# A spectral filter beside an MLP block on one core: four more warm-up matmuls and another order in step one

## The chip, the cores and the metric

The kernel runs on one NeuronCore of a Trainium2 chip. Its engines are called as in the profile: PE multiplies matrices (PEld is its loading of weights), DVE, ACT and POOL work element by element, SP issues the DMAs. The metric is the time of one execution on the device in microseconds. Lower is better.

## The reference

For x of 2048 tokens by 448 features, with all numbers in float32:

```python
xn = layernorm(x)
out = x + A(xn, w_r, w_i) + B(xn, w1, w2, w3, w4)

def A(x, w_r, w_i):                       # a filter in the frequency domain
    X = rfft2(x) * (w_r + 1j * w_i)       # over tokens and features
    return irfft2(X)

def B(x, w1, w2, w3, w4):
    h = gelu(layernorm(x) @ w1)
    hs = shift(h) @ w2                    # quarters of h moved by +1, -1, +2, -2 tokens
    x1 = x + hs
    return x1 + gelu(layernorm(x1) @ w3) @ w4
```

w3 is 448 by 1792 and w4 1792 by 448. gelu is its tanh form.

## The kernel before

Tokens lie in 16 blocks b of 128 rows: row a of block b is token 16 a + b + 2 (modulo 2048). Two blocks share a tile `xt[p]`, p = b // 2, of 128 by 2 by 448 float32 numbers, on which all results are added up. Float32 matrices are multiplied in three float16 passes: each operand is split into a high half, made by ACT, and a low half, the rest, made by DVE (`PASS`: high by high, high by low, low by high).

The kernel is one stream of instructions per engine. A scheduler lays out each engine's order when the kernel is built, by priorities and by edges written out by hand, and the chip then executes every engine's list strictly in that order. `behind(key)` is such an edge: what is issued in its block comes, on each engine, after the instruction of the same engine noted under that key. It orders an engine's queue and is no wait between engines. Waits between engines come from the data alone.

The stages, in order of time:

1. Start. `warm_up(WARM)` multiplies zeros (`wps`), while x and the weights are loaded. Then the first layer norm (`norm1`), sums of squares of w1 from which a power of two as its scale is found (`powers`, pm, L259), transposes of x on PE (L384), the product with w1 (L415), gelu, the shift, the product with w2 (`w2_tile`, L474). All loads and the transposes by DMA go through SP's queue.
2. The second layer norm, `ln2`, once for two or four blocks: DVE's statistics, centred copies by POOL and ACT (L495, L497), then for each block a scaled high half by ACT (L504), a low half by DVE (L505, L507) and a transpose by DMA (L509) into `x2all`. The last call is for blocks 12 to 15. Pairs 6 and 7 of the MLP read them.
3. The MLP over pairs G of blocks. Its unit (G, fp), fp 0 to 6, has two parts. `front` multiplies with w3 (L395, 22 matmuls of 256 columns into one bank), then come gelu (L724) and the halves hf by ACT (L726) and DVE (L727). `back` multiplies hf with w4 and sums up in two banks acc (L806, 12 matmuls of 448 columns). The fronts run two units ahead of the backs (`AH`). When fp is 6, DVE adds acc to `xt` (L813), which frees the banks. The unit's ACT and DVE instructions are noted as ("f", G, fp), its last matmul as ("m", G, fp). `mlp([0])` comes first, then `mlp([1, 2])`, then the others beside the later stages.
4. Step one of the transform, beside `mlp([1, 2])`. `do_fold(b)` loads x again for two blocks (xf), normalises it (ACT, L536), and POOL folds the features (L542 to L545) into f. `step1_in` splits f into xh (ACT L552, DVE L553), four buffers. `step1(b)` multiplies it with the transform over the 128 rows (L562, 12 matmuls into a bank ps), and ACT (L566) and DVE (L567) write the two halves y. There are two banks ps, so that each pair of blocks needs those of the pair before emptied. `PACE` says behind the last matmul of which unit the pair of blocks 2 i and 2 i + 1 is multiplied, `FOLD` behind which unit it is folded.
5. Also beside `mlp([1, 2])`: `unscale(p)` loads x once more (loads, two halves of a staging space) and sets xt[p] = xt[p] * scale + x on DVE (L515), for p 1 to 7. `w_scale` loads the filter's eight parts (wl, two halves of another space) and takes the largest magnitude of each on DVE (`absmax`, L270 by its helper). `w_scale_end` makes a power of two from the eight. `w4_sums` prepares three parts of w4 for a later stage.
6. The 16 chunks of the transform over tokens with the filter (`chunk_a`, `chunk_b`, `chunk_z`, `chunk_c`) beside pairs 3 and 4, the inverse (`inv_a`, `inv_b`), and pairs 5 to 7 of the MLP.

What sets the order around the change: `between`, called after each front of `mlp([1, 2])`, issues an unscaling or a part of w4 behind the unit that `EARLY` names. The maxima stand behind the units of `WMAX`. The loads' DMAs are issued in program order with no edge, and SP executes its list in order.

Of the kernel before, what the change touches and what calls it, by code (L numbers as in the profile page):

```python
# [25 lines left out]
TURN = [3, 1, 0, 2]  # L26
DONE = {c: [c - 2] for c in range(2, 12)} | {12: [10, 13], 13: [11, 12, 14, 15]}
FIRST = 2
WARM = 24
ZPRE = 2.0 ** -7  # L30
UPRE = 2.0 ** -3
VPRE = 2.0 ** -3
EPS = 1e-5
AH = 2
PACE = [(1, 0), (1, 1), (1, 2), (1, 4), (1, 5), (2, 0), (2, 1), (2, 3)]
FOLD = [(0, 6), (1, 0), (1, 1), (1, 3), (1, 4), (1, 6), (2, 0), (2, 2)]
PIN = [("a3",), ("a3",), ("a3",), ("a3",)]
WMAX = [(1, 4), (1, 5), (1, 6), (2, 0), (2, 1), (2, 2), (2, 3), (2, 4)]
EVAC, FILL = 0, 100000
DH = D // 2  # L40
SEVEN = {5: [0, 4, 5], 6: [0, 4, 5, 1, 2, 3], 7: [0, 1, 2, 4, 5]}
# [83 lines left out]
def body(tc, nc, x, wf, w1, w2, w3, w4, c_g, c_n, c_small, out):  # L125
# [50 lines left out]
    def stage(name, n, side, dtype=F32):  # L176
        t = pw.tile([128, 1808], F32, tag=f"stage{side}", bufs=1, name=name)
        return (t if dtype is F32 else t.bitcast(dtype))[:, :n]
# [90 lines left out]
    def absmax(out_, in_):  # L269
        V.tensor_reduce(out=out_, in_=in_, axis=AX.X, op=ALU.max, apply_absolute_value=True)  # L270
# [98 lines left out]
    @contextlib.contextmanager  # L369
    def behind(*key):  # L370
        key = key if len(key) > 1 else key[0]
        with contextlib.ExitStack() as st:
            for i in after[key]:
                st.enter_context(tc.issue_after(i))
            yield
# [99 lines left out]
        V.scalar_tensor_tensor(out=xb(b), in0=xb(b), scalar=cs[:, CS[b]:CS[b] + 1], in1=pm[:, :D],  # L475
                               op0=ALU.mult, op1=ALU.add)

    def ln2(bs, engines):

        n, b0 = len(bs), bs[0]  # L480
        mv = stats([xb(b) for b in bs], f"b{b0}")
        a = pc.tile([128, 4], F32, tag="vb", bufs=2, name=f"vb{b0}")[:, :n]
        r = pc.tile([128, 4], F32, tag="vs", bufs=2, name=f"vs{b0}")[:, :n]
        o, y = [], []
        nm = pc.tile([128, 4], F32, tag="nm", bufs=2, name=f"nm{b0}")[:, :n]
        P.tensor_scalar(out=nm, in0=mv[:, :n, 0], scalar1=-1.0, scalar2=None, op0=ALU.mult)
        for m in range(0, n, 2):
            w = stage(f"y{b0 + m}", 8 * 448, (b0 + m) // 2 % 2, F16)
            o.append(w[:, 0:4 * D].bitcast(F32).rearrange("p (i n) -> p i n", i=2))
            y.append(w[:, 4 * D:8 * D].rearrange("p (i n) -> p i n", i=2))  # L490
            for i in range(2):
                e = engines[m + i]
                c = nm[:, m + i:m + i + 1]
                if e is A:
                    A.activation(out=o[-1][:, i], in_=xb(b0 + m + i), func=AF.Identity, bias=c)  # L495
                else:
                    e.tensor_scalar(out=o[-1][:, i], in0=xb(b0 + m + i), scalar1=1.0, scalar2=c,  # L497
                                    op0=ALU.mult, op1=ALU.add)
        V.tensor_scalar(out=a, in0=mv[:, :n, 1], scalar1=eps12, scalar2=None, op0=ALU.add)
        rsqrt(r, a, n, f"b{b0}")  # L500
        for i in range(n):
            b, h, x_ = b0 + i, y[i // 2][:, i % 2], o[i // 2][:, i % 2]
            k = r[:, i:i + 1]
            u = A.activation(out=h[:, 0:D], in_=x_, func=AF.Copy, scale=k)  # L504
            V.scalar_tensor_tensor(out=h[:, 448:512], in0=x_[:, 384:448], scalar=k, in1=h[:, 384:448],  # L505
                                   op0=ALU.mult, op1=ALU.subtract)
            v = V.scalar_tensor_tensor(out=h[:, 512:896], in0=x_[:, 0:384], scalar=k, in1=h[:, 0:384],  # L507
                                       op0=ALU.mult, op1=ALU.subtract)
            d = SY.dma_start_transpose(out=x2all[b // 4][:, :, 128 * (b % 4):128 * (b % 4) + 128], in_=h)  # L509
            after[f"b{b0}"] = u.ins, v.ins, d.ins  # L510

    def unscale(p, part):
        t = part.rearrange("p (b n) -> p b n", b=2)
        SY.dma_start(t, xv[:, at_token(2 * p):at_token(2 * p) + 2])
        return lambda: V.scalar_tensor_tensor(out=xt[p], in0=xt[p], scalar=p12, in1=t, op0=ALU.mult, op1=ALU.add)  # L515
# [40 lines left out]
    def step1(b):  # L556
        t = xh_buf[b % 4]
        pm = bank("sp", f"ps1_{b}")
        for q in range(4):
            for n, (xi, ri) in enumerate(PASS):  # L560
                o = xi * 452 + 113 * q
                T.matmul(pm[:, 128 * q:128 * q + 128], t[:, o:o + 128], cR[ri][:, 128 * (q % 2):128 * (q % 2) + 128],  # L562
                         start=n == 0, stop=n == 2)
        src = pm.rearrange("p (q h k) -> p q h k", h=2, k=4)
        y = [Ya[:, p, :, :, :, b, :].rearrange("p q c h k -> p (q c) h k") for p in range(2)]
        A.activation(out=y[0], in_=src, func=AF.Copy)  # L566
        V.tensor_tensor(out=y[1], in0=src, in1=y[0], op=ALU.subtract)  # L567

    sc = pc.tile([128, 4], F32, name="sc")

    def w_scale():
        wm = pc.tile([128, 8], F32, name="wm")
        t = stage("wl", 8 * DF, 1)
        for c in range(8):
            h = t[:, 4 * DF * (c % 2):4 * DF * (c % 2) + 4 * DF]
            SY.dma_start(h, wf.rearrange("c (p r) n -> (c p) (r n)", r=8)[:, 4 * DF * c:4 * DF * (c + 1)])
            with behind("f", *WMAX[c]):
                absmax(wm[:, c:c + 1], h)
        return wm

    def w_scale_end(wm):
        t = pc.tile([128, 4], F32, name="wt")
        V.tensor_reduce(out=t[:, 0:1], in_=wm, axis=AX.X, op=ALU.max)
        pt = bank("sp", "wpt")
        T.transpose(pt[0:1, 0:128], t[:, 0:1], ident)
        V.tensor_reduce(out=t[0:1, 1:2], in_=pt[0:1, 0:128], axis=AX.X, op=ALU.max)
        V.tensor_scalar(out=t[0:1, 1:2], in0=t[0:1, 1:2], scalar1=2.0 ** -20, scalar2=None, op0=ALU.max)
        pb = bank("sp", "wpb")
        T.matmul(pb[:, 0:1], ones[0:1], t[0:1, 1:2], start=True, stop=True)
        e = pc.tile([128, 3], I32, name="we")  # L590
        V.tensor_copy(out=t[:, 2:3], in_=pb[:, 0:1])
        V.tensor_single_scalar(e[:, 0:1], t.bitcast(I32)[:, 2:3], 0x7F800000, op=ALU.bitwise_and)
        V.tensor_single_scalar(e[:, 1:2], e[:, 0:1], 0x7F800000, op=ALU.bitwise_xor)
        V.tensor_scalar(out=sc[:, 0:1], in0=e.bitcast(F32)[:, 1:2], scalar1=ZPRE, scalar2=None, op0=ALU.mult)
        for h in range(2):
            V.tensor_scalar(out=sc[64 * h:64 * h + 64, 2:3], in0=sc[64 * h:64 * h + 64, 0:1], scalar1=2.0 * h - 1.0,
                            scalar2=None, op0=ALU.mult)
        V.tensor_scalar(out=sc[:, 1:2], in0=e.bitcast(F32)[:, 0:1], scalar1=2.0 ** -21 / (ZPRE * UPRE * VPRE),
                        scalar2=s12[:, 0:1], op0=ALU.mult, op1=ALU.mult)
        V.tensor_scalar(out=sc[:, 3:4], in0=sc[:, 1:2], scalar1=p12, scalar2=None, op0=ALU.mult)  # L600
# [146 lines left out]
    def w4_sums(j, part):  # L747

        t = part.rearrange("p (k n) -> p k n", n=DH)
        SY.dma_start(t.rearrange("p (f k) n -> p f (k n)", f=2), w4v[:, 2 * j:2 * j + 2])  # L750

        def go():
            for o, i, k, op in ((3, 3, 1, ALU.subtract), (1, 1, 0, ALU.subtract),
                                (0, 3, 0, ALU.add), (2, 2, 0, ALU.subtract)):
                V.tensor_tensor(out=t[:, o], in0=t[:, i], in1=t[:, k], op=op)
            split_w(w4t[j][:, 0], w4t[j][:, 1], t, s4)
        return go
# [228 lines left out]
    ln2(range(8, 12), [P, A, P, A])  # L986
    for b in range(12, 16):
        w2_tile(b)
    ln2(range(12, 16), [P, A, P, A])
    close("p1")  # L990
    close("pr")

# [6 lines left out]
    for i in range(4):  # L999
        P.memset(xh_buf[i][:, 904:], 0.0)  # L1000
    loads = stage("loads", 1808, 0)
    EARLY = {(1, 0): 1, (1, 1): 2, (1, 3): 3, (1, 5): 4, (1, 6): 5, (2, 1): 6, (2, 2): 7,
             (2, 3): "4", (2, 4): "5", (2, 5): "0"}

    def between(G, fp):
        if (G, fp) in EARLY:
            k, n = EARLY[G, fp], list(EARLY).index((G, fp))
            part = loads[:, 896 * (n % 2):896 * (n % 2) + 896]
            go = w4_sums(int(k), part) if isinstance(k, str) else unscale(k, part)
            with behind("f", G, fp):  # L1010
                go()

    mlp([1, 2], hook=between, ahead=AH, tags=("mm", "tr"))
    for b in range(0, NB, 2):
        do_fold(b)
        step1_in(b)
        step1_in(b + 1)
        with behind("m", *PACE[b // 2]):
            step1(b)
            step1(b + 1)  # L1020
    with behind("X", 14):
        wm = w_scale()
    close("pfd")
    with behind("m", 2, 4):
        w_scale_end(wm)
    pst = pool("pst", side="right")
    zb = [pst.tile([128, 4 * DF + 16], F16, name=f"zb{i}") for i in range(2)]
    for i in range(2):
# [64 lines left out]
```

## Time and profile before

| | us |
|---|---|
| three runs | 412.36, 412.37, 414.42 |
| median | 412.37 |
| the profiled execution | 414.05 |
| its span, first to last instruction | 412.2 |

The profile is of one execution, the one of 414.05 us. All times of its rows are counted from the start of its span. The page's first part gives busy times and their share of the span. A row of the timeline has the start, the duration, the engine, the line of the kernel, the operation, what it writes and reads, and a count where like instructions are merged; in brackets stands how long the engine had been idle and what ended that. A group has its busy time, the mean of one in ns, and the idle time ahead of it. A line of the waits has the engine, what it waited for, the sum in us, how often, and the longest. A helper's line stands for all its callers.

### The profile page before, as it was taken

How to read it: one execution, taken by the hardware profiler on the slowest of the kernel's cores; microseconds unless marked ns; L12 is line 12 of the kernel's file. 1: busy time of each engine (PE TensorE's matmuls, PEld its weight loads, DVE VectorE, ACT ScalarE, POOL GpSimd, SP SyncE). 2: the span in 40 equal slices, each digit the busy share in tenths (PEclk: the TensorE clock that was granted, in tenths of full speed). 3: DMA queues.
4: the chain of work that ended last, by engine and by line, in shares of the span. 5: the costliest groups of instructions: out<-in, count | busy, mean ns of one | idle time of the engine just before them, and what ended most of it. 6: DMA issues, size and time to landing. Idle time of an engine off the chain costs nothing.

```text
span 412.2 us, 8724 instructions
## 1 busy us (share of the span) xinstructions
PE 401.3 (97%) x3389; PEld 298.0 (72%) x3389; DVE 333.9 (81%) x702; ACT 255.8 (62%) x434; POOL 100.9 (24%) x173
## 2 busy tenths in 40 slices
PE   6999999999999999999999999999999999999996
PEld 2655545755658677777787888877777779998995
DVE  5878998999775858987798888956799998966645
ACT  4679789982567857565498888954453453553331
POOL 7688520110035866420011221110000000000000
PEclk9899999999999999999999999999999999999999
DMA  8976985479297557435355556610021012100101
GB/s 272 377 278 128 245 170 146 81 122 198 54 238 208 173 173 233 139 131 143 84 147 152 147 142 161 163 32 14 0 91 68 25 67 82 56 23 0 46 2 45
DMA packets 54596, 52.07 MB, mean 126 GB/s; under 512 B 35678, under 2 KB 48542, under 8 KB 54556
## 3 DMA queue, kind: packets, MB, share of 16 engines
q1 hardware_dynamic: 54556, 51.53, 46.0%
q8 instruction: 26, 0.43, 0.4%
q14 instruction: 14, 0.11, 0.1%
HBM read 38.28 MB, written 3.67 MB: 102 GB/s over the span
## 4 chain that ended last, share of the span: by engine, by line
PE 60%; DMA 2%; issue 1%; DVE 1%; POOL 0%; SPq 0%
PE pw L395 24%; PE acc L806 16%; PE side L776 4%; PE acc L776 3%; PE pu L665 3%; PE pe L686 2%; PE pp L620 2%; PE px L637 2%; PE py L707 2%; DMA wl<-wf 2%; PE ps L562 1%; DVE wm L270 0%; POOL xr L543 0%; POOL f L545 0%; DVE y L567 0%
## 5 line engine op out<-in xcount | busy, mean ns | idle before, releaser
L395 PE MATMUL pw<-x2mem,w3p 128*128 128x256 f16 x1232 | 150.6, 273 | 0.0
L395 PEld LDWEIGHTS <-w3p 128*128 128x128 f16 x1232 | 119.3, 98 | 19.9
L806 PE MATMUL acc<-w4p,hf 128*128 128x448 f16 (+1 forms) x516 | 105.6, 348 | 0.7 <-ACT hf L726 0.7
L806 PEld LDWEIGHTS <-hf 128*128 128x128 f16 x516 | 49.6, 98 | 37.6 <-ACT hf L726 1.0
L724 ACT ACTIVATE pw<-pw,pe 128x512 f32<-128x512 f32 x42 | 27.4, 653 | 29.4 <-PE pw L395 29.4
L727 DVE SCALAR_TENSOR_TENSOR hf<-pw,h,hf 128x512 f16<-128x512 f32 x42 | 31.3, 745 | 12.8 <-ACT hf L726 12.7
L415 PE MATMUL pw<-w1p,xT 128*128 128x448 f16 x176 | 35.5, 356 | 1.1 <-DVE xT L389 0.6
L474 PE MATMUL pw<-w2p,h 128*128 128x448 f16 x176 | 35.6, 353 | 0.9 <-DMA h<-x2mem 0.8
L646 POOL TENSOR_TENSOR z<-te 128x450 f32<-128x450 f32 x16 | 15.7, 982 | 70.3 <-DVE te L644 70.3
L415 PEld LDWEIGHTS <-xT 128*128 128x128 f16 x176 | 17.2, 99 | 18.3 <-ACT xT L388 1.2
L726 ACT ACTIVATE hf<-pw,h 128x512 f16<-128x512 f32 x42 | 28.8, 686 | 1.8 <-PE acc L806 0.8
L474 PEld LDWEIGHTS <-h 128*128 128x128 f16 x176 | 16.9, 98 | 17.1 <-DMA h<-x2mem 2.3
L742 ACT ACTIVATE hz<-g,h 128x896 f16<-128x896 f32 x14 | 14.6, 1042 | 22.6 <-DVE g L739 22.5
L776 PEld LDWEIGHTS <-hz 128*128 128x128 f16 x294 | 28.2, 98 | 0.4
L627 ACT ACTIVATE pf<-pp 64x450 f16<-64x450 f32 x32 | 17.4, 543 | 12.4 <-DVE pf L628 8.0
L628 DVE TENSOR_TENSOR pf<-pp,pf 64x450 f16<-64x450 f32 x32 | 19.9, 622 | 3.4 <-ACT pf L627 3.0
L743 DVE SCALAR_TENSOR_TENSOR hz<-g,h,hz 128x896 f16<-128x896 f32 x14 | 16.1, 1149 | 7.6 <-ACT hz L742 7.6
L553 DVE TENSOR_TENSOR xh<-f,xh 128x452 f16<-128x452 f32 x16 | 12.4, 809 | 7.4 <-ACT xh L552 7.4
L642 ACT ACTIVATE te<-px 64x450 f32<-64x450 f32 x32 | 17.3, 541 | 1.2 <-DMA wc<-wf 0.5
L545 POOL TENSOR_TENSOR f<-xr 128x452 f32<-128x452 f32 x16 | 17.5, 1116 | 0.6
L736 ACT ACTIVATE g<-pw,pe 128x512 f32<-128x512 f32 x14 | 9.5, 681 | 10.1 <-PE pw L395 10.0
L690 ACT ACTIVATE e<-pe 128x226 f32<-128x226 f32 x16 | 5.8, 360 | 16.0 <-DVE vh L700 9.0
(188 smaller groups left out, 716.5 us busy)
## 6 DMA issues: line engine op xcount, KB each, us to landing
wc<-wf SPq DMA_DIRECT2D x32, 225.0 KB, 3.6
wl<-wf SPq DMA_DIRECT2D x8, 450.0 KB, 4.2
xt<-x SPq DMA_DIRECT2D x8, 448.0 KB, 7.4
xf<-x SPq DMA_DIRECT2D x8, 448.0 KB, 3.7
loads<-x SPq DMA_DIRECT2D x7, 448.0 KB, 4.2
out<-xt SPq DMA_DIRECT2D x13, 224.0 KB, 1.9
w3raw<-w SPq DMA_DIRECT2D x3, 896.0 KB, 11.1
gn<-c_g SPq DMA_DIRECT2D x16, 128.0 KB, 3.1
```

The source lines that it names most:

```text
L395: T.matmul(ps_out, wp[:, wi + t, cols], xT[:, xi + t, tok], start=t == 0 and wi + xi == 0, stop=t == 3 and wi == 4)
L415: T.matmul(pm[:, :D], xTs[g][:, xi + t, 128 * i:128 * i + 128], w1p[:, wi + t], start=t == 0 and p == 0, stop=t == 3 and p == 2)
L474: T.matmul(pm[:, :D], h[:, k], w2p[:, w], start=n == 0, stop=n == 10)
L545: P.tensor_tensor(out=f[:, :, k:k + 2].rearrange("p b s d -> p s b d"), in0=u[:, :, 0], in1=u[:, :, 1], op=op)
L627: A.activation(out=hi, in_=src, func=AF.Copy)
L628: V.tensor_tensor(out=lo, in0=src, in1=hi, op=ALU.subtract)
L642: A.activation(out=e[64 * h:64 * h + 64], in_=px_[64 - 64 * h:128 - 64 * h, :2 * DF], func=AF.Copy)
L724: A.activation(out=pm, in_=pm, func=AF.Gelu_apprx_tanh, scale=r3)
L726: i = A.activation(out=h[:, 0], in_=pm, func=AF.Copy, scale=h3)
L727: j = V.scalar_tensor_tensor(out=h[:, 1], in0=pm, scalar=h3, in1=h[:, 0], op0=ALU.mult, op1=ALU.subtract)
L776: m = T.matmul(to, h[:, hi, 128 * blk:128 * blk + 128], b[wi], start=new and n == 0, stop=n == 2 and (last if blk in (2, 5, 3, 0) else end ...
L806: m = T.matmul(to, h[:, hi, o:o + 128], w4p[0][:, wi, f, r], start=first and f % 2 == 0 and n == 0, stop=end and f % 2 == 1 and n == 2, sk ...
```

## The change

Six edits.

- `WARM` is 28 in place of 24.
- `PACE`: the first five pairs are multiplied a unit later, (1, 1), (1, 2), (1, 3), (1, 5), (1, 6) in place of (1, 0), (1, 1), (1, 2), (1, 4), (1, 5). The last three keep their units.
- The unscalings of tiles 3 to 7 and the eight maxima leave the units of `EARLY` and `WMAX`. They are issued right after a pair of step one, on DVE behind the low half y of the pair's second block: none for the pair 0, tile 3 behind the pair 1, up to tile 7 behind the pair 5 (`AFTER`); part 0 behind the pair 0, then 1, 2, 3 and 4, 5, 6, 7 (`WMAX`). Their loads are issued at the same place of the program. Tiles 1 and 2 stay behind the units (1, 0) and (1, 1).
- `w4_sums` of the parts 4, 5 and 0 stays behind the units (2, 3), (2, 4) and (2, 5).
- `w_scale_end` comes behind the last matmul of (2, 3) in place of (2, 4).
- The last call of `ln2` has its four scaled copies (L504) behind the ACT instruction of the unit (0, 6).

```diff
-WARM = 24
+WARM = 28
-PACE = [(1, 0), (1, 1), (1, 2), (1, 4), (1, 5), (2, 0), (2, 1), (2, 3)]
+PACE = [(1, 1), (1, 2), (1, 3), (1, 5), (1, 6), (2, 0), (2, 1), (2, 3)]
-WMAX = [(1, 4), (1, 5), (1, 6), (2, 0), (2, 1), (2, 2), (2, 3), (2, 4)]
+WMAX = [[0], [1], [2], [3, 4], [5], [6], [7], []]
+AFTER = [[], [3], [4], [5], [6], [7], [], []]
...
-    def ln2(bs, engines):
+    def ln2(bs, engines, late=None):
...
-            u = A.activation(out=h[:, 0:D], in_=x_, func=AF.Copy, scale=k)
+            with behind(*late) if late else contextlib.nullcontext():
+                u = A.activation(out=h[:, 0:D], in_=x_, func=AF.Copy, scale=k)
...
-        V.tensor_tensor(out=y[1], in0=src, in1=y[0], op=ALU.subtract)
+        after["y", b] = (V.tensor_tensor(out=y[1], in0=src, in1=y[0], op=ALU.subtract).ins,)
...
-    def w_scale():
-        wm = pc.tile([128, 8], F32, name="wm")
-        t = stage("wl", 8 * DF, 1)
-        for c in range(8):
-            h = t[:, 4 * DF * (c % 2):4 * DF * (c % 2) + 4 * DF]
-            SY.dma_start(h, wf.rearrange("c (p r) n -> (c p) (r n)", r=8)[:, 4 * DF * c:4 * DF * (c + 1)])
-            with behind("f", *WMAX[c]):
-                absmax(wm[:, c:c + 1], h)
-        return wm
+    def w_scale(t, c):
+        h = t[:, 4 * DF * (c % 2):4 * DF * (c % 2) + 4 * DF]
+        SY.dma_start(h, wf.rearrange("c (p r) n -> (c p) (r n)", r=8)[:, 4 * DF * c:4 * DF * (c + 1)])
+        absmax(wm[:, c:c + 1], h)
+
+    wm = pc.tile([128, 8], F32, name="wm")
...
-    ln2(range(12, 16), [P, A, P, A])
+    ln2(range(12, 16), [P, A, P, A], ("f", 0, 6))
...
-    EARLY = {(1, 0): 1, (1, 1): 2, (1, 3): 3, (1, 5): 4, (1, 6): 5, (2, 1): 6, (2, 2): 7,
-             (2, 3): "4", (2, 4): "5", (2, 5): "0"}
+
+    def half(n):
+        return loads[:, 896 * (n % 2):896 * (n % 2) + 896]
 
     def between(G, fp):
-        if (G, fp) in EARLY:
-            k, n = EARLY[G, fp], list(EARLY).index((G, fp))
-            part = loads[:, 896 * (n % 2):896 * (n % 2) + 896]
-            go = w4_sums(int(k), part) if isinstance(k, str) else unscale(k, part)
+        if (G, fp) in ((1, 0), (1, 1)):
+            go = unscale(fp + 1, half(fp))
             with behind("f", G, fp):
                 go()
 
     mlp([1, 2], hook=between, ahead=AH, tags=("mm", "tr"))
+    wl = stage("wl", 8 * DF, 1)
     for b in range(0, NB, 2):
         do_fold(b)
         step1_in(b)
...
         with behind("m", *PACE[b // 2]):
             step1(b)
             step1(b + 1)
-    with behind("X", 14):
-        wm = w_scale()
+        with behind("y", b + 1):
+            for p in AFTER[b // 2]:
+                unscale(p, half(p + 1))()
+            for c in WMAX[b // 2]:
+                w_scale(wl, c)
+    for n, j in enumerate((4, 5, 0)):
+        go = w4_sums(j, half(n))
+        with behind("f", 2, 3 + n):
+            go()
     close("pfd")
-    with behind("m", 2, 4):
-        w_scale_end(wm)
+    with behind("m", 2, 3):
+        w_scale_end()
```

In the changed kernel's lists PE has the same matmuls but for the four. On ACT the gelu and the high half of (0, 6) come ahead of the last four copies, and the gelu of (1, 0) ahead of the first xh. On DVE the low halves y of a pair come ahead of the unscaling and the maximum that follow the pair. On SP the first two loads wl come ahead of the third load for unscaling.

More of the change, by code (lines that the diff above doesn't have):

```diff
@@ L566, in step1, with w_scale_end @@
         A.activation(out=y[0], in_=src, func=AF.Copy)
-        V.tensor_tensor(out=y[1], in0=src, in1=y[0], op=ALU.subtract)
+        after["y", b] = (V.tensor_tensor(out=y[1], in0=src, in1=y[0], op=ALU.subtract).ins,)
     sc = pc.tile([128, 4], F32, name="sc")
-    def w_scale():
-        wm = pc.tile([128, 8], F32, name="wm")
-        t = stage("wl", 8 * DF, 1)
-        for c in range(8):
-            h = t[:, 4 * DF * (c % 2):4 * DF * (c % 2) + 4 * DF]
-            SY.dma_start(h, wf.rearrange("c (p r) n -> (c p) (r n)", r=8)[:, 4 * DF * c:4 * DF * (c + 1)])
-            with behind("f", *WMAX[c]):
-                absmax(wm[:, c:c + 1], h)
-        return wm
-    def w_scale_end(wm):
+    def w_scale(t, c):
[3 more added lines that the diff above has]
+    wm = pc.tile([128, 8], F32, name="wm")
+    def w_scale_end():
         t = pc.tile([128, 4], F32, name="wt")
```

## The prediction

> **What bounds the kernel now.** I read the page first, then PE by stages, then what ended PE's idle times, then the order of time around each of them.
>
> ```profile
> span 412.2 us, 8724 instructions
> PE 401.3 (97%) x3389; PEld 298.0 (72%) x3389; DVE 333.9 (81%) x702; ACT 255.8 (62%) x434; POOL 100.9 (24%) x173
> ```
> ```profile
> 7.50:10.90 3.40, 1.19 (x9) 0.71 (x7) 2.05 (x8) 2.14 (x7) 1.14 (x2) 1.00 1.02 323
> 10.90:14.35 3.45, 3.45 (x17) 2.79 (x16) 3.00 (x9) 3.23 (x7) 1.25 (x2) 0.51 1.05 331
> ```
> ```profile
> 161.65:192.90 31.25, 31.25 (x289) 24.23 (x289) 28.20 (x45) 17.94 (x30) 9.18 (x10) 1.00 0.41 131
> 192.90:404.30 211.40, 211.40 (x2053) 173.83 (x2051) 171.23 (x324) 120.39 (x202) 15.72 (x16) 1.00 0.27 77
> 404.30:412.20 7.90, 4.58 (x37) 3.28 (x34) 3.31 (x6) 1.35 (x2) 0.00 (x0) 1.00 0.17 58
> ```
> ```profile
> PE pm L259 <- DVE pt L257: 2.2, 1, 2.2
> PE ps L562 <- DVE y L567: 1.4, 2, 0.9
> PE acc L806 <- ACT hf L726: 0.7, 1, 0.7
> ```
>
> In the rows by stage the columns are the length, the busy time of PE, weight loads, DVE, ACT and POOL, the granted clock, the DMA share and GB/s. PE is the bound: from 161.65 to 404.30 it isn't idle for a moment, so whatever makes PE reach that point earlier shortens the kernel by as much, as long as its inputs come earlier too. PE is idle 412.2 - 401.3 = 10.9 us. Of this 3.3 lie in the last 7.90 us, 1.2 before the first matmul and 2.2 before the first sum (pm), which waits for the squares of w1 and not for PE. Two other waits are what this change touches: 0.7 at an acc and 1.4 at the ps of step one. About 2.0 us of idle lie elsewhere. Besides, PE ran at half clock (0.51) from 10.90 to 14.35, though it was busy all that time. In the 3.4 us before, it had been busy for 1.19.
>
> **The change part by part: warm-up.** Four matmuls more before the first sum.
>
> ```profile
> 1.22 6.76 PE L836 MATMUL wps<-wsrc 128*128 128x512 f16 x24 [1.22 <-DVE wsrc L191]
> 2.05 0.15 PEld L836 LDWEIGHTS <-wsrc 128*128 128x128 f16 x1 [0.28 <-issue]
> 2.48 0.15 PEld L836 LDWEIGHTS <-wsrc 128*128 128x128 f16 x1 [0.27 <-issue]
> 4.15 3.34 PEld L836 LDWEIGHTS <-wsrc 128*128 128x128 f16 x16 [0.24 <-issue]
> 10.19 0.38 PE L259 MATMUL pm<-pt,ones 128*128 128x1 f32 x2 [2.21 <-DVE pt L257]
> 10.44 3.21 PE L384 MATMUL pta<-ident,xt 128*128 128x128 f32 x16
> 13.44 2.88 PE L415 MATMUL pw<-w1p,xT 128*128 128x448 f16 x12
> 20.33 0.71 POOL L333 TENSOR_SCALAR xt<-xt,vy,nma 128x448 f32<-128x448 f32 x1
> 22.35 1.94 PE L384 MATMUL pta<-ident,xt 128*128 128x128 f32 x16
> 26.05 8.11 PE L415 MATMUL pw<-w1p,xT 128*128 128x448 f16 x41 [0.29 <-DVE xT L389]
> ```
>
> The last sixteen follow each other every 3.34 / 16 = 0.21 us, the early ones every 2.48 - 2.05 = 0.43. Four more take 0.84, or 1.72 at the slow pace. PE would be done at 8.8 or 9.7 instead of 7.98, ahead of 10.19 in both cases: the wait for pt hides them. If pt came 1 us earlier, the slow four would cost 0.5.
>
> What they can bring is the half clock. Sixteen transposes took 3.21 us in it and 1.94 outside (1.27 lost). Twelve products with w1 took 2.88 against 12 x 8.11 / 41 = 2.37 (0.51 lost). That is 1.8 at most. With the four, PE is busy for 1.19 + 0.84 = 2.03 of those 3.4 us, 60% in place of 35%. That 35% lost the full clock is in the row; whether 60% keeps it, no row shows, so the lower end is nothing. The next transposes, at 22.35, can't begin before POOL's normalised block at 20.33 + 0.71 = 21.04, so 1.3 of it can pass through and the last 0.5 only if POOL moves too. I take **1.7**: the profiled execution took 414.05 us (1.85 lies around its span), the runs 412.36, 412.37 and 414.42, and the two low ones lie 1.68 below it, like executions without that stretch. This is an inference.
>
> The Trainium skill (TensorE: Matmul & The Clock Gate, Part 1: The HAM clock gate) says that the clock follows PE's activity in a free-running window of 3413 ns. The 3.45 us at 0.51 agree. By its statement in Part 4 (PE-mode transpose) that transposes don't count as busy, the window would hold only the warm-up, and the sum would be rival A's. This trace speaks against that: the clock came back at 14.35 after a stretch that was mostly transposes.
>
> **The last copies.** The four copies of the last second norm now stand behind the unit (0, 6) on ACT.
>
> ```profile
> 116.64 2.33 ACT L504 ACTIVATE y<-y,vs 128x448 f16<-128x448 f32 x4
> 118.88 0.63 ACT L724 ACTIVATE pw<-pw,pe 128x512 f32<-128x512 f32 x1
> 119.54 0.69 ACT L726 ACTIVATE hf<-pw,h 128x512 f16<-128x512 f32 x1
> 120.29 2.48 PE L806 MATMUL acc<-w4p,hf 128*128 128x448 f16 x12 [0.69 <-ACT hf L726]
> 125.97 1.05 ACT L552 ACTIVATE xh<-f 128x452 f16<-128x452 f32 x2 [4.20 <-POOL f L545]
> 128.93 2.43 PE L806 MATMUL acc<-w4p,hf 128*128 128x448 f16 x12
> ```
>
> Gelu and hf pass 2.33 us of copies, so hf is there near 118 and the wait of **0.7** goes. The copies come 1.3 later, and with them the lo halves on DVE, the four transposes on SP and the loads queued behind these. The transposes feed pairs 6 and 7 of the MLP, hundreds of us later. The first load of x for unscaling is due at DVE behind hf(1, 0), later than before by nothing, so that its cover shrinks by these 1.3. ACT's first fold stays about where it is, since it followed both before. Late next would be hf(1, 0): it stands behind xh, which waits for POOL, while PE reaches its acc 0.7 earlier than 128.93. In the new order its gelu is ahead of xh, which gives 0.6 back. The price stays between 0 and 0.7 gained; I take 0.7.
>
> **The pairs.** Eight pairs are multiplied behind units (1, 1) to (2, 3); the last keeps its place, so the tail isn't pushed.
>
> ```profile
> 135.85 2.39 DVE L553 TENSOR_TENSOR xh<-f,xh 128x452 f16<-128x452 f32 x2 [1.04 <-ACT xh L552]
> 138.17 0.68 DVE L567 TENSOR_TENSOR y<-ps,y 128x512 f16<-128x512 f32 x1
> 138.90 0.83 PE L562 MATMUL ps<-csm,xh 128*128 128x128 f16 x12 [0.85 <-DVE y L567]
> ```
> ```profile
> 155.67 4.22 DMA wl<-wf
> 159.91 1.09 DVE L270 TENSOR_REDUCE wm<-wl 128x1 f32<-128x900 f32 x1 [1.28 <-DMA wl<-wf]
> 160.92 1.28 DVE L567 TENSOR_TENSOR y<-ps,y 128x512 f16<-128x512 f32 x2
> 161.65 1.50 PE L562 MATMUL ps<-csm,xh 128*128 128x128 f16 x24 [0.56 <-DVE y L567]
> ```
>
> Both waits are for a bank of the pair before, whose lo half stood late in DVE's queue: once behind two xh, once behind a maximum that waited for its load (the chain of waits runs through that 4.22). In the new order the y's of a pair stand ahead of the maxima and unscalings, and a pair has a whole unit to be emptied: 0.85 + 0.56 = **1.4** gained, at best.
>
> Whether DVE keeps up I read from the groups and from PE's pitch.
>
> ```profile
> L553 DVE TENSOR_TENSOR xh<-f,xh 128x452 f16<-128x452 f32 x16 | 12.4, 809 | 7.4 <-ACT xh L552 7.4
> L567 DVE TENSOR_TENSOR y<-ps,y 128x512 f16<-128x512 f32 x16 | 10.5, 681 | 0.9 <-ACT y L566 0.9
> L515 DVE SCALAR_TENSOR_TENSOR xt<-xt,s,loads 128x896 f32<-128x896 f32 x7 | 9.3, 1334 | 0.0
> L270 DVE TENSOR_REDUCE wm<-wl 128x1 f32<-128x900 f32 x8 | 8.7, 1084 | 1.7 <-DMA wl<-wf 1.7
> L727 DVE SCALAR_TENSOR_TENSOR hf<-pw,h,hf 128x512 f16<-128x512 f32 x42 | 31.3, 745 | 12.8 <-ACT hf L726 12.7
> ```
> ```profile
> 144.24 1.50 PE L562 MATMUL ps<-csm,xh 128*128 128x128 f16 x24
> 150.25 2.57 PE L395 MATMUL pw<-x2mem,w3p 128*128 128x256 f16 x22
> ```
>
> A pair with its unit takes PE 150.25 - 144.24 = 6.0 us. DVE needs 1.6 (two xh) + 1.4 (two y) + 0.7 (hf) + 1.3 (one unscaling) + 1.1 (one maximum) = 6.1. That is no slack in a full pair, but five of the eight are full pairs (one of them with two maxima), two carry a maximum only and the last carries nothing, and the units (1, 4) and (2, 2) have no pair. The work itself isn't changed. On SP the first two loads of the filter (wl) move ahead of the third load of x and wait for the last transposes, whose source lay in their space; the third load of x waits behind them, but isn't needed before the second pair. Later maxima get their loads one or two pairs ahead, which is more than 4.22.
>
> **The sum.** 414.05 - 1.7 - 0.7 - 1.4 = 410.25. From the median of the runs, 412.37, without the first term: 412.37 - 2.1 = 410.27.
>
> **The rivals.** A: the half clock stays, because 60% isn't enough or the window falls otherwise. For it: only 35% and 100% are shown. Against it: 60% is nearer to what the two low runs would have. 414.05 - 2.1 = 411.95.
>
> B: the pairs' gain is taken by a new wait. After the acc of (1, 6) PE has the pair and the products with w3 of a unit (6.0 less 2.4 for an acc, 3.6 us) before the acc of (2, 0) needs the banks. DVE has one unscaling and two maxima (1.3 + 2 x 1.1 = 3.5) and then the additions to xt that free them. For it: if DVE started on these only as the acc ends, it would be late. Against it: it can start when the pair before is emptied, some 4 us sooner. 410.25 + 1.4 = 411.65.
>
> C, slower: the maxima block DVE. They now stand fixed between the y's and the next hf, and their loads go through SP, in order, behind loads that wait for POOL. If each of five full pairs waits 1.28 as at 159.91, and a full pair has no slack, PE gets 5 x 1.28 = 6.4: 416.65. It makes the kernel slower than its median from 2.1 us of such waits on. Against it: the loads have a pair's lead, and two units without a pair give 4.6 us each to catch up (6.0 less 1.4 for a pair's products).
>
> **How the numbers follow.** A measurement of this kernel can tell about 0.5% from no change, that is below 410.31 or above 414.43. Forecast 0.64, A 0.11, B 0.10, C 0.15. The forecast sits on the edge. I count 0.50 of it as faster, because the 2.0 us of other idle time can only add to the gain, and 0.14 as no change. With A and B: faster 0.50, same 0.35, slower 0.15. The range goes down to 409.0 (somewhat more than half of those 2.0 us) and up to A with the copies' 0.7 back, 412.6. It leaves C out, and some 0.05 at the bottom.
>
> **What would show it.** Right: a granted clock of 1.00 from 10.9 to 14.35, no idle time ahead of the acc of (0, 6), none ahead of any ps, and PE without idle time from about 130. Wrong: 0.5 in that stretch (A); an acc of (2, 0) that waits for the additions to xt (B); idle DVE ahead of maxima with acc or ps waiting behind (C). The forecast fails as a whole if PE is ahead at 160 and the gain is gone at 300, which would mean that another engine sets the pace of the chunks.

## The result and the profile after

| | before | after |
|---|---|---|
| median of 7 runs | 412.37 us (412.04 to 414.42) | 410.26 us (409.98 to 410.94) |
| profiled execution: time, span, mean granted clock | 414.05, 412.2, 0.996 | 410.06, 408.4, 1.000 |

The ratio is 0.9941 with an interval of 0.9925 to 0.9958: 0.6% faster. The profiled execution gained 3.99 us and the median 2.11, largely because the profiled execution of before ran a stretch at half clock that only part of the executions of before have. 3.45 us at half clock are 0.4% of 412 us. So a mean granted clock of 0.996 or less is taken as the sign of such a stretch; the other executions show 0.998 to 1.000. The mean doesn't say where in the kernel the stretch lies.

The profile after opens with the span and the busy time of the engines.

```profile
span 408.4 us, 8753 instructions
PE 400.2 (98%) x3393; PEld 297.1 (73%) x3393; DVE 334.7 (82%) x702; ACT 254.9 (62%) x434; POOL 100.8 (25%) x173
```

Next the view by stages (length, busy time of PE, weight loads, DVE, ACT and POOL, granted clock, DMA share, GB/s).

```profile
7.50:10.90 3.40, 2.31 (x16) 1.40 (x14) 2.27 (x11) 2.12 (x8) 1.14 (x2) 1.00 1.02 334
10.90:14.35 3.45, 3.45 (x24) 2.25 (x23) 3.05 (x7) 3.45 (x8) 1.56 (x3) 1.00 1.05 354
131.20:161.65 30.45, 30.45 (x279) 22.97 (x277) 24.01 (x29) 22.66 (x42) 24.37 (x22) 1.00 0.55 190
```

PE is busy for 2.31 of the 3.40 us ahead of 10.90, where it was 1.19, and the next 3.45 us have the full clock. The stretch with the pairs, 131.20 to 161.65, has no idle time on PE. The waits of PE in the same execution (us in total, times, longest):

```profile
PE pw L475 <- DMA h<-x2mem: 1.4, 3, 0.8
PE wps L835 <- DVE wsrc L192: 1.2, 1, 1.2
PE pm L260 <- DVE pt L258: 1.1, 1, 1.1
```

No wait of acc for hf and none of ps for y is left; the longest total is now a load of h. The order of time on PE shows where the lead over before grows.

```profile
20.59 1.94 PE L385 MATMUL pta<-ident,xt 128*128 128x128 f32 x16
...
35.00 1.31 PE L475 MATMUL pw<-w2p,h 128*128 128x448 f16 x6 [0.85 <-DMA h<-x2mem]
...
40.66 1.68 PE L416 MATMUL pw<-w1p,xT 128*128 128x448 f16 x8
...
112.70 4.70 PE L805 MATMUL acc<-w4p,hf 128*128 128x448 f16 x24
...
186.42 2.56 PE L396 MATMUL pw<-x2mem,w3p 128*128 128x256 f16 x22
```

The same places in the order of time before:

```profile
36.07 1.31 PE L474 MATMUL pw<-w2p,h 128*128 128x448 f16 x6 [0.15 <-DMA h<-x2mem]
...
41.88 0.35 PE L415 MATMUL pw<-w1p,xT 128*128 128x448 f16 x1
...
114.02 4.70 PE L806 MATMUL acc<-w4p,hf 128*128 128x448 f16 x24
...
190.37 0.82 PE L395 MATMUL pw<-x2mem,w3p 128*128 128x256 f16 x6
```

The lead is 22.35 - 20.59 = 1.76 us at the second transposes, 1.22 at 40.66, since PE now waits 0.85 for a load of h where it waited 0.15, 1.32 at 112.70, 3.95 at 186.42, and 412.2 - 408.4 = 3.8 at the end. So 2.6 us come between 113 and 186: the waits of 0.69, 0.85 and 0.56, and the overlap that each stop costs besides (two halves of a ps group take 0.83 + 0.83 where an unbroken one takes 1.50). With it the three stops cost 0.9, 1.0 and 0.7. VectorE (DVE in the rows; ScalarE is ACT and GpSimd is POOL) around the first pair, after:

```profile
133.11 2.39 DVE L555 TENSOR_TENSOR xh<-f,xh 128x452 f16<-128x452 f32 x2 [1.65 <-ACT xh L554]
135.43 0.74 DVE L726 SCALAR_TENSOR_TENSOR hf<-pw,h,hf 128x512 f16<-128x512 f32 x1
136.63 1.29 DVE L569 TENSOR_TENSOR y<-ps,y 128x512 f16<-128x512 f32 x2 [0.47 <-ACT y L568]
137.83 1.08 DVE L271 TENSOR_REDUCE wm<-wl 128x1 f32<-128x900 f32 x1
```

Both y of the pair stand together at 136.63, ahead of the maximum; before, two xh of 2.39 us stood between them.

### The profile page after: what moved, and what is told of

Read it like the earlier page. It is cut to its first block, busy times and chain, and to the rows that moved or that the text cites. A ratio compares the mean times of both kernels' runs of the same rounds, so it can differ in the third digit from the quotient of the medians.

```text
span 408.4 us, 8753 instructions
## 1 busy us (share of the span) xinstructions
PE 400.2 (98%) x3393; PEld 297.1 (73%) x3393; DVE 334.7 (82%) x702; ACT 254.9 (62%) x434; POOL 100.8 (25%) x173
## 4 chain that ended last, share of the span: by engine, by line
PE 84%; DMA 4%; ACT 3%; POOL 3%; DVE 3%; issue 2%; SPq 0%; ACTq 0%; POOLq 0%; DVEq 0%
PE pw L396 31%; PE acc L805 23%; PE pw L475 6%; PE side L775 4%; PE acc L775 3%; PE pu L664 3%; PE ps L564 3%; PE pe L685 2%; PE pp L619 2%; PE px L636 2%; PE pw L416 2%; PE py L706 2%; DMA h<-x2mem 2%; DMA w1s<-w 1%; DVE w3p L280 1%
## 5 line engine op out<-in xcount | busy, mean ns | idle before, releaser
L547 POOL TENSOR_TENSOR f<-xr 128x452 f32<-128x452 f32 x16 | 19.7, 1250 | 0.6
L555 DVE TENSOR_TENSOR xh<-f,xh 128x452 f16<-128x452 f32 x16 | 14.2, 914 | 6.2 <-ACT xh L554 6.2
L544 POOL TENSOR_TENSOR xr<-xf 128x452 f32<-128x452 f32 x8 | 9.2, 1152 | 21.8 <-issue 16.0
```

The costliest lines, as they stand in the source:

```text
L547: P.tensor_tensor(out=f[:, :, k:k + 2].rearrange("p b s d -> p s b d"), in0=u[:, :, 0], in1=u[:, :, 1], op=op)
```

## The experiments

All of these are one of the two kernels with the edit shown. "Stretch" counts the executions with a mean clock of 0.996 or less, wherever it was lost. Kernel before, measured beside them: 413.04, 412.64 and 412.51 on three occasions; 24 of its 71 executions had the stretch, with a median of 413.53 against 412.43 for the other 47. That is 1.1 us for the stretch. Without it the three occasions gave 412.43, 412.49 and 412.32, so that medians of different occasions can be compared to about 0.2 us.

| kernel | warm-up | pairs later | pins | copies' edge | median us | stretch | ratio to before |
|---|---|---|---|---|---|---|---|
| before_warm28 | 28 | no | no | no | 412.19 | 0 of 12 | 0.998 (0.9967 to 0.9993) |
| pairs_as_before | 28 | no | no | yes | 411.85 | 1 of 12 | 0.9972 (0.9958 to 0.9987) |
| pins_only | 28 | no | yes | no | 411.62 | 0 of 12 | 0.9973 (0.9962 to 0.9984) |
| later_only | 28 | yes | no | no | 413.76 | 4 of 12 | 1.0034 (1.0019 to 1.0049) |
| copies_free | 28 | yes | yes | no | 412.24 | 0 of 12 | 0.998 (0.9969 to 0.9991) |
| after_oldpace | 28 | no | yes | yes | 410.24 | 0 of 6 | 0.9937 (0.9922 to 0.9951) |
| after_again | 28 | yes | yes | yes | 410.52 | 0 of 6 | 0.9945 (0.993 to 0.996) |
| after_warm24 | 24 | yes | yes | yes | 410.75 | 0 of 6 | 0.9944 (0.9928 to 0.9961) |
| after_warm24_again | 24 | yes | yes | yes | 410.31 | 2 of 6 | 0.9953 (0.9936 to 0.9971) |
| after_warm16 | 16 | yes | yes | yes | 411.56 | 10 of 12 | 0.9967 (0.9954 to 0.998) |

Two more kernels, copies_free_y_first (411.41, 0.9971, 0.9956 to 0.9986) and unpinned (416.61, 1.0099, 1.0081 to 1.0118), are described below. "Pins" stands for the maxima and unscalings at their new places behind y, with `w_scale_end` moved as in the change.

**The warm-up.** The kernel before with the four matmuls alone, and the changed kernel without them:

```diff
-WARM = 24
+WARM = 28
```

> The kernel before with 28 warm-up matmuls and nothing else. Theory: all executions have a clock of 0.999 to 1.000; none is near 414, the median is about 412.2, the lowest as before at 412.0. So the median hardly moves, and what the warm-up takes away is the slow executions. Rival (the warm-up gives its 1.7 us in every execution): the median falls to 410.7.

> The changed kernel with 24 warm-up matmuls again. Theory (the four matmuls keep the clock full by filling the idle time before the first sum): with 24 some executions have a mean clock of 0.996 and are 1.2 to 1.8 us longer than the others, which stand near 410.0 with a clock of 1.000; the spread of the runs is over 1.2 us, where 28 gave 409.98 to 410.94. Rival (the half clock of the profiled execution before was chance, and 28 changes nothing in it): the runs look as with 28, within 1 us, or 28 and 24 show 0.996 alike.

The four matmuls alone bring 412.19, with none of 12 executions in the stretch where the kernel before had 12 of 29 on the same chip. Taking them out of the changed kernel gave 410.75, with a spread of 1.23 us but no execution in the stretch, so that these six show no cost of a lost clock. To tell how often the clock falls, 24 were tried again, and 16:

> The changed kernel with 24 warm-up matmuls a second time, to tell how often the clock falls. Theory 1 (24 matmuls end too early in some executions, as in the kernel before: a mean clock of at most 0.996 in 17 of its 48 executions so far, against 2 of 63 in kernels with 28 or more): in 3 to 8 of some 10 executions the mean clock is 0.996 or less, and these are about 1.1 us longer; median 410.6 (410.3 to 411.4). Theory 2 (the changed kernel's start needs no more than 24): none does, 410.4 (410.1 to 410.8).

> The changed kernel with 16 warm-up matmuls in place of 28. Theory 1 (the share of busy time in the 3.4 us ahead of 10.9 us decides the clock of the next 3.45 us: 1.19 busy lost it, 2.31 kept it): with 16 the warm-up ends about 2 us earlier than with 24, busy time there falls to 0.5 or less, and most executions have the half clock: at least 12 of 15 with a mean clock below 0.998, median 411.4 (411.0 to 411.8). Theory 2 (the start counts for nothing by the end, since the matmuls wait for the load of h at 35 us anyway): 410.3 (410.0 to 410.6), with the mean clock below 0.998 as well.

With 16, ten of twelve executions had the stretch (three of them at 0.992), and the median rose to 411.56; the two without it took 410.32 and 410.34. With 24 it was 2 of 12 over both occasions; these two took 411.31 and 411.53, the other four of that occasion 410.1 to 410.33. The granted clock shows where it changes. In the profiled execution of before it is half from 10.93 to 14.34, which is 3.41 us. With 16 matmuls it is half from 9.20 to 16.03, twice that length:

```profile
5.79:9.20 3.41, 1.29 (x6) 0.39 (x4) 3.24 (x12) 2.50 (x7) 2.50 (x3) 1.00 1.04 350
9.20:12.61 3.41, 2.45 (x12) 2.45 (x13) 1.08 (x8) 1.59 (x5) 1.12 (x2) 0.50 1.06 320
12.61:16.03 3.42, 3.42 (x14) 2.10 (x13) 3.42 (x7) 3.42 (x8) 1.18 (x3) 0.50 1.05 355
```

So in these traces the clock holds for whole lengths of 3.41 us, and where they begin differs from execution to execution. The stretch from 7.50 to 10.90 is such a length in before (7.51 to 10.93) and nearly one in after, but not here. In the profiled execution of after_warm24_again the clock falls at 408.05, behind the last matmul. Counted back from there by 117 lengths of 3.413 us, the one with the idle time ahead of the first sum is this:

```profile
8.69:12.11 3.42, 2.06 (x18) 2.02 (x19) 1.78 (x8) 2.26 (x6) 1.15 (x3) 1.00 1.05 331
```

2.06 busy of 3.42 (60%) kept the clock, as did 2.33 (68%) in after; 1.21 (35%) in before and 1.29 (38%) with 16 had lost it. From 10.29 on, for 1.82 of the 2.06, they are transposes, so transposes count as busy here. That the lengths begin elsewhere in each execution would explain why only some executions lose the clock. It is an argument and not shown, since only one execution of each run was profiled. With 16, 6.83 us at half clock make 6.83 x 0.5 / 410.8 = 0.8%, the mean clock of 0.992.

**The copies' edge.** The changed kernel without it:

```diff
-    ln2(range(12, 16), [P, A, P, A], ("f", 0, 6))
+    ln2(range(12, 16), [P, A, P, A])
```

> The changed kernel without the edge on the last four copies. Theory (the copies ahead of the unit (0, 6) cost PE its 0.69 at the acc): 410.9, and the trace has the wait of acc for hf near 118 again, 0.7 long. Rival (the gain is absorbed before the first pair, since hf(1, 0) waits for the fold): 410.3 as with the edge.

The whole gain over before_warm28 is gone: 412.24. But the wait of acc (0, 6) for hf isn't back. In the order of time, first ScalarE (from pins_only, whose copies are free too, at the old place), then PE:

```profile
114.86 2.33 ACT L506 ACTIVATE y<-y,vs 128x448 f16<-128x448 f32 x4
117.09 0.63 ACT L723 ACTIVATE pw<-pw,pe 128x512 f32<-128x512 f32 x1
117.76 0.69 ACT L725 ACTIVATE hf<-pw,h 128x512 f16<-128x512 f32 x1
```
```profile
118.50 2.47 PE L805 MATMUL acc<-w4p,hf 128*128 128x448 f16 x12
```

The copies stand ahead of gelu and hf as before, and no wait of acc is listed: they start at 114.86, and not at 116.64 as in the profiled execution of before, while PE is only about 1 us earlier. hf ends at 118.45 and acc starts at 118.50, so it comes just in time; about 0.2 us are lost there all the same (first column of the table below). What copies_free has in its place is on VectorE, at the first pair:

```profile
137.84 0.69 DVE L569 TENSOR_TENSOR y<-ps,y 128x512 f16<-128x512 f32 x1 [0.71 <-ACT y L568]
138.90 2.38 DVE L555 TENSOR_TENSOR xh<-f,xh 128x452 f16<-128x452 f32 x2 [0.37 <-ACT xh L554]
141.21 0.68 DVE L569 TENSOR_TENSOR y<-ps,y 128x512 f16<-128x512 f32 x1
```
```profile
142.03 0.83 PE L564 MATMUL ps<-csm,xh 128*128 128x128 f16 x12 [1.10 <-DVE y L569]
```

Two xh of the next pair stand between the two y, and PE waits 1.10 us. If this order is the cause, setting it by hand must bring the time back without the edge:

```diff
-        step1_in(b)
-        step1_in(b + 1)
+        with behind("y", 1) if b == 4 else contextlib.nullcontext():
+            step1_in(b)
+            step1_in(b + 1)
```

> The changed kernel without the edge on the copies, but with the two xh of the second pair ordered behind the y of the first. Theory 1 (the edge does not bring its own 0.7 us of waiting; it turns the order on VectorE, so that y of pair 0 stands ahead of two xh): the wait of ps for y of 1.10 us in that kernel goes, and 412.2 comes down by about that, to 411.1 (410.8 to 411.4) or lower. Theory 2 (the edge counts by the place of the copies themselves, ahead of the last slice of the first pass): the time stays at 412.2 (411.9 to 412.5) whatever VectorE's order is. If the order is all that the edge brings, it comes to 410.3.

411.41: 0.83 of the 1.7 to 2.0 us to the changed kernel. The wait at that pair went, and waits of 0.20 and 0.50 came at the next one (0.7 in total). So the order on VectorE is worth about half of what the edge brings by this run, and ordering one pair by hand moves part of the stall to the next pair. Whether the order is all of it, this run doesn't show.

**The pairs, the pins and the edge apart.** First the copies' edge with the 28 matmuls, on the kernel before:

```diff
-    ln2(range(12, 16), [P, A, P, A])
+    ln2(range(12, 16), [P, A, P, A], ("f", 0, 6))
```

> The kernel before with 28 warm-up matmuls and the edge on the copies, but pairs, maxima and unscalings as before. Theory (the pairs' part is worth 0.85 + 0.56 = 1.4): 411.7, with PE waits for y at two ps again. If the pairs' part is worth nothing: 410.3. If it is worth all of the 2.1: 412.4.

411.85. Of the two waits of ps, the first is gone (both y of the first pair stand together at 131.69) and the second is there as in before:

```profile
157.16 1.09 DVE L270 TENSOR_REDUCE wm<-wl 128x1 f32<-128x900 f32 x1 [0.29 <-DMA wl<-wf]
158.17 1.28 DVE L568 TENSOR_TENSOR y<-ps,y 128x512 f16<-128x512 f32 x2
```
```profile
158.90 1.50 PE L563 MATMUL ps<-csm,xh 128*128 128x128 f16 x24 [0.55 <-DVE y L568]
```

Then the changed kernel with the old units, the changed kernel as its measure on the same chip, and each of the two other parts alone with 28 matmuls: the new units on the kernel before (later_only), and the pins with old units and free copies (pins_only).

```diff
-PACE = [(1, 1), (1, 2), (1, 3), (1, 5), (1, 6), (2, 0), (2, 1), (2, 3)]
+PACE = [(1, 0), (1, 1), (1, 2), (1, 4), (1, 5), (2, 0), (2, 1), (2, 3)]
```

> The changed kernel once more, as the measure for the three that follow on one chip. Expected: 410.3 us (410.0 to 411.0), no wait of ps for y and none of acc for hf.

> The changed kernel with the old units for step one's first five pairs; the maxima and unscalings stay pinned behind y, the copies and the 28 matmuls stay. Theory 1 (the later unit is what removes the waits of ps for y; the pins only keep VectorE free for y): about 411.4 (411.0 to 411.8), with waits of ps for y of 0.5 to 1.4 us in the trace. Theory 2 (the pins alone remove the waits, and the later unit does nothing): 410.3 (410.0 to 410.6) and no wait of ps for y.

> The kernel before with 28 warm-up matmuls and the first five pairs a unit later, nothing else. Theory 1 (the later unit by itself does nothing for y, since the scheduler lets the other work of VectorE go ahead of it): 412.2 (411.9 to 412.6), with waits of ps for y of 0.5 us or more in the trace. Theory 2 (the prediction: the later unit ends the waits): 411.2 (410.8 to 411.5) and no such wait.

> The kernel before with 28 warm-up matmuls and the pins of maxima and unscaling behind y alone: old units for the pairs, copies without their edge. Theory 1 (the pins keep VectorE free for y, whatever the unit; the edge on the copies adds only what it added to the kernel before, 0.35 us): 410.6 (410.2 to 411.0), and at most one short wait of ps for y. Theory 2 (as with the later units, VectorE's order without the edge costs 1.9 us): 412.2 (411.8 to 412.5), with waits of ps for y of about 1 us.

With the old units the changed kernel takes 410.24, 410.52 with the new: the later unit is worth nothing there, against the first theory, and no wait of ps for y is in the trace. Alone it is slower than both theories had it, 413.76. Without the four executions with a low clock it is 413.50, 1.3 us above before_warm28. Its VectorE and PE:

```profile
138.11 0.68 DVE L567 TENSOR_TENSOR y<-ps,y 128x512 f16<-128x512 f32 x1
139.68 2.39 DVE L553 TENSOR_TENSOR xh<-f,xh 128x452 f16<-128x452 f32 x2 [0.89 <-ACT xh L552]
141.99 0.68 DVE L567 TENSOR_TENSOR y<-ps,y 128x512 f16<-128x512 f32 x1
```
```profile
142.82 0.83 PE L562 MATMUL ps<-csm,xh 128*128 128x128 f16 x12 [1.94 <-DVE y L567]
```

Two xh stand between the y's again, and the wait is 1.94 in place of the 0.86 of before_warm28, whose two waits are these:

```profile
137.47 0.83 PE L562 MATMUL ps<-csm,xh 128*128 128x128 f16 x12 [0.86 <-DVE y L567]
159.85 1.50 PE L562 MATMUL ps<-csm,xh 128*128 128x128 f16 x24 [0.18 <-DVE y L567]
```

The longer wait isn't the whole 1.3. The last 36 matmuls, first in later_only and then in before_warm28:

```profile
402.68 4.73 PE L806 MATMUL acc<-w4p,hf 128*128 128x448 f16 x36
```
```profile
402.35 4.73 PE L806 MATMUL acc<-w4p,hf 128*128 128x448 f16 x36
```

They start only 0.33 later. From there to the end of the span it is 411.7 - 402.68 = 9.0 us in place of 410.4 - 402.35 = 8.05, and for this 1.0 the runs show no cause.

The pins alone lie between the two theories, 411.62: their one wait of ps for y (0.85) is the first pair's, and the second has gone. Across the traces of eight kernels the rule is the same: in the three with the edge (after, pairs_as_before, after_oldpace) both y of the first pair stand together, in the five without it (before, before_warm28, later_only, pins_only, copies_free) two xh stand between them.

Where the time goes is seen from the starts on PE of the same matmuls. The kernels with the old units have the same matmuls between these places; the times are us of the profiled execution:

| kernel | acc of 24 near 113 to acc (1, 0) | on to acc (1, 2) | on to acc (1, 6) |
|---|---|---|---|
| before | 14.91 | 13.04 | 23.42 |
| before_warm28 | 14.19 | 13.04 | 23.05 |
| pairs_as_before (edge) | 14.01 | 12.03 | 23.41 |
| pins_only | 14.17 | 13.03 | 22.71 |
| after_oldpace (edge and pins) | 14.01 | 12.09 | 22.70 |

The first column holds the acc of (0, 6), the second the first wait of ps, the third the second wait. Against before_warm28 the edge gains 0.18 and 1.0 in the first two and loses 0.36 in the third: PE comes earlier and waits 0.55 there in place of 0.18. The pins alone gain 0.34, in the third. With both it is 1.48, and nothing is lost there.

Last, whether it is the pin or the place of the maxima and unscalings in the program:

```diff
-        with behind("y", b + 1):
+        if True:
```

> The kernel with old units, copies' edge and 28 matmuls, and the maxima and unscalings issued at their new places but without the edge that pins them behind y. On VectorE's order the maxima of several slices then stand together, ahead of y. Theory 1 (it is the pin that gives the gain): slower than 410.24 by 1 us or more, with waits of ps for y, and maxima that wait for their loads. Theory 2 (the new places alone give it): 410.2 (410.0 to 410.6).

This is after_oldpace without the pin: 416.61. VectorE and PE:

```profile
126.68 1.14 DVE L517 SCALAR_TENSOR_TENSOR xt<-xt,s,loads 128x896 f32<-128x896 f32 x1
133.15 1.09 DVE L271 TENSOR_REDUCE wm<-wl 128x1 f32<-128x900 f32 x1 [5.33 <-DMA wl<-wf]
134.16 0.74 DVE L726 SCALAR_TENSOR_TENSOR hf<-pw,h,hf 128x512 f16<-128x512 f32 x1
```
```profile
134.96 2.06 PE L805 MATMUL acc<-w4p,hf 128*128 128x448 f16 x10 [1.37 <-DVE hf L726]
...
140.67 0.27 PE L564 MATMUL ps<-csm,xh 128*128 128x128 f16 x2 [2.34 <-DVE y L569]
```

A maximum stands at the head of VectorE's queue for 5.33 us until its load lands. hf and y are queued behind it, and PE waits for both. It is the mechanism of rival C, as one long wait and not five short ones; that the time is close to C's 416.65 is chance.

Not all of the 6.4 us to after_oldpace are such waits, which come to about 4.2 in the trace. Behind them the clock falls as well:

```profile
139.10:142.52 3.42, 1.47 (x19) 1.07 (x19) 3.42 (x6) 0.00 (x0) 1.52 (x3) 1.00 0.94 334
142.52:145.93 3.41, 3.41 (x22) 2.46 (x20) 3.41 (x4) 1.86 (x3) 2.62 (x2) 0.50 0.97 329
```

PE was busy for 1.47 of 3.42 us (43%), and the next 3.41 ran at half clock, which is at most 1.7 us. All four executions have a mean clock of 0.996, though the start of the profiled one has the full clock.

## Why the prediction came true, point by point

**The bound** was right: the lead of 3.95 us at 186 is 3.8 at the end, so no other engine set the pace later.

**The warm-up: right in mechanism, too large.** The row that was wanted is there, 1.00 from 10.90 to 14.35. The term of 1.7 measured 1.76 at the second transposes (0.30 of it was there before the first transposes, at 10.14 in place of 10.44, as pt came earlier), but 1.1 at the end (413.53 less 412.43): in the profiled executions the lead shrinks when PE waits for the load of h. The step that took the distance of the low runs from the profiled execution for the price of the stretch took the size too high. The inference behind it holds: a third of before's executions have the stretch (24 of 71), and without it they take 412.43. Rival A is out, since 68% kept the clock in after. Its time of 411.95 was no good sign in any case: it starts from the profiled execution, while by the prediction's own inference the median execution of before had no stretch to lose. That 28 matmuls are needed in the changed kernel, and not 24, rests on 2 of 12 against none of 19 (7, 6 and 6 executions of after, after_again and after_oldpace) and isn't settled. later_only had a low clock in 4 of 12 with 28, but it needn't have been lost at the start. Of a length of 3.41 us around its stop of 1.94 only 1.47 are busy, the share that lost the clock in unpinned. Its profiled execution kept the clock, so that this isn't shown.

**The copies: the step failed.** The wait of 0.7 that it was to end is in the one profiled execution of before, with the stretch; in the profiles of before_warm28, copies_free and pins_only the copies are as early in ScalarE's order and no wait of acc (0, 6) is listed; the edge saves about 0.2 there. What the edge changes is the order that the scheduler gives VectorE at the first pair, and with it the 0.85 that the prediction had booked under the pairs.

**The pairs: the sum was right, its cause was wrong.** 0.85 + 0.56 are both gone. But "a pair has a whole unit to be emptied" isn't why: with the old units they are gone too, and the later unit alone makes the first wait 1.94. The edge on the copies ends the first wait and the pins end the second. From 412.19 the edge brings 0.34 and the pins 0.57 alone; both together bring 1.95. Of the 2.0 us between the profiled executions of before_warm28 and after_oldpace, 1.48 are in the three columns of the table, and 0.56 is already there at the acc of 24 near 113 us (113.31 against 112.75), in a part of the program that the edits don't touch. Why the two together bring more than their sum, 1.95 against 0.91, is shown for 0.3 of it, by the second wait that grows with the edge alone. The rest is open: the profiled execution of pairs_as_before (411.29) was the fastest of its twelve and says little of the median.

**The sum.** 3.8 against a measured 3.99 for the profiled execution: 1.32 at the start (for 1.7), 0.90 up to the acc of (1, 0) (for 0.7) and 1.73 at the pairs (for 1.4). For the medians it is 2.1 against 2.11. There the terms make up for each other: the copies give about 0.2 by their own place, the pairs' waits went with more overlap than was counted, and part of the gain lies ahead of 113 us. That the sum fits to 0.01 is luck.

**Rivals B and C.** B's place, the acc of (2, 0), has no wait in the trace after. C's wait isn't there either: no maximum waits for a load ahead of a y. Without the pin it comes, at 416.61.

## What to carry to other kernels

An edge given to a scheduler can change the order of other engines behind it: take each part of a change alone and in pairs before crediting it, for here one of three parts brought nothing with the others and made a wait longer alone. An instruction that waits for a load should stand behind what the bounding engine waits for on the same queue. A wait found in one profiled execution may belong to executions of that kind only; compare its mean clock with those of other executions before counting it in a median, and look in the trace for the place where the clock was lost.

## What the runs showed of the hardware

The two xh took 2.39 us in some places and 1.17 in others. In pins_only, VectorE and then GpSimd:

```profile
134.05 2.40 DVE L555 TENSOR_TENSOR xh<-f,xh 128x452 f16<-128x452 f32 x2 [1.05 <-ACT xh L554]
...
138.88 1.17 DVE L555 TENSOR_TENSOR xh<-f,xh 128x452 f16<-128x452 f32 x2 [0.17 <-ACT xh L554]
```
```profile
133.48 1.07 POOL L544 TENSOR_TENSOR xr<-xf 128x452 f32<-128x452 f32 x1
134.50 1.46 POOL L545 TENSOR_TENSOR xr<-xf 128x452 f32<-128x452 f32 x1
136.04 2.19 POOL L547 TENSOR_TENSOR f<-xr 128x452 f32<-128x452 f32 x2
139.54 1.43 POOL L544 TENSOR_TENSOR xr<-xf 128x452 f32<-128x452 f32 x1 [1.31 <-issue]
```

The slow pair ran beside GpSimd's work. Of the fast pair the first xh ran in the pause ahead of 139.54; the second ran beside L544 and kept its time, but that instruction took 1.43 us where it took 1.07 at 133.48. In these rows the one that starts later is the one that takes longer. All 82 xh over 0.8 us in the fourteen traces ran beside a GpSimd instruction. The Trainium skill (GPSIMD Engine Reference, 8. Key points) says that GpSimd shares its SBUF interfaces with VectorE and contends with instructions that have two SBUF inputs; xh has two, and these rows agree. So two xh ahead of a y hold it for 2.4 us and not 1.2 where GpSimd is busy. No run here moved GpSimd's work alone.
